# Scores of the global queries made once a batch from a ring of four key tiles, with a builder that counts TensorE's instruction records and with new ranks of the tasks

## The chip, the cores and the metric

The kernel runs on one core of one Trainium2 chip. The core has five engines that run their own instruction lists and wait for each other through semaphores: TensorE (PE in the profile; its weight loads are PEld), VectorE (DVE), ScalarE (ACT), GpSimd (POOL) and SyncE (SP), which here issues all the DMAs. PE writes into PSUM, eight banks of 128 partitions by 512 fp32 numbers; the other data lie in SBUF. The metric is the device time of one execution in microseconds (us).

## The reference

The reference computes attention and then two feed-forward layers on its output:

```python
# attention: batch 4, heads 8, 512 local rows, 32 global rows, head size 64
s_g   = scale * q_g @ concat(k_g, k_l).T            # 32 global queries see all 544 keys
out_g = softmax(s_g) @ concat(v_g, v_l)
s_ll  = where(|i - j| <= 32, scale * q_l @ k_l.T, -1e9)   # local queries: a band ...
s_l   = concat(scale * q_l @ k_g.T, s_ll)                 # ... and the 32 global keys
out_l = softmax(s_l) @ concat(v_g, v_l)
x = concat(out_g, out_l)                            # 2176 rows of 512
# layer 1: rms norm, then (silu(x @ w_gate) * (x @ w_val)) @ w_out, inner size 1536
# layer 2: (sigmoid(x @ w_gate2) * (x @ w_val2)) @ w_out2
```

The weights come as 64-bit floats and are turned into pairs of fp16 numbers (a high and a low part) on the chip.

## The kernel before, in words

The 512 local rows of each batch are four tiles of 128 rows, so there are 16 tiles, T = 0 to 15. A tile goes through a chain of tasks. SP loads its queries, keys and values (`lq`, `lk`, `lv`). PE transposes keys and queries (`k`, `q`), and ACT or DVE copies them out of PSUM into the tile's `kT` and `qT` (`kc`, `qc`). PE makes the banded scores (`a1`: 8 products with a mask, 32 score products of 128 columns), DVE takes the maxima (`mx`), ACT the exponentials (`ex`), PE transposes them (`a2`), ACT or DVE copies them (`pc`), PE multiplies with the value windows `vw` (`a3`, 16 products for each half of the heads), DVE divides (`nm`), ACT, POOL and DVE normalise (`sq`, `ms`, `sc`), PE transposes once more (`a4`), and `xh`, `xl` split the result into the fp16 tiles `xhi`, `xlo`. Each task from `mx` to `nm` exists twice for a tile, for the even and the odd heads (e = 0, 1).

The global queries need every tile of their batch. Before, `st_sg` makes, tile by tile, 16 fp32 products of 64 columns (20 in the last tile of a batch, four of them with the global keys), taking the even and the odd heads in turn; `st_sgc` copies the two results into an SBUF tile `sg`. After the fourth tile `g1` takes the maximum of the whole row on DVE, `g1x` the exponential and the sum on ACT, and `g2`, `gc`, `g3`, `gn`, `gx` transpose, copy, multiply with the values, divide and write to `xG`. The key tiles `kT` come from a pool of three buffers.

The matrix products of layer 1 are cut into pieces of six (`gemm`; tile `wgv` holds gate and value weights, `wo` the output weights). The first two of its twelve weight groups run during attention, as pieces between the attention tasks. A piece needs its three tiles' `xl` and the converted weights. All later products come after attention in a fixed order.

The order on each engine is set when the program is built. `attend` keeps a clock for each engine (`now`), and `book` adds a cost for each instruction. `choose` looks at all tasks whose predecessors have been issued, takes the engine with the earliest possible start, and on it, among those that can start within a short look-ahead (`LOOK`), the task with the lowest rank: a number in units of tiles that is written into `tile_tasks`, `batch_tasks` and `W_PRIO`. A piece of a product has rank 1000, so it stands behind every attention task that can start. Where the builder's clock shows PE waiting for more than `FILL` = 500 ns, it puts in products that nobody uses, fillers (`b<-ident 128x256` in bf16), one for each 110 ns. On the chip each engine executes its list strictly in order, so a task that was put too early holds up everything behind it.

Of the kernel before, what the change touches and what calls it, by code (L numbers as in the profile page):

```python
# [21 lines left out]
def tile_attention_moe_moe(  # L22
# [21 lines left out]
    def tag_of(x):  # L44
        n = x.tensor.name
        return (n, x.offset) if n.startswith(("xhi", "xlo", "ya")) else n
# [13 lines left out]
    mode = [None]  # L60

    class Booked:
# [4 lines left out]
        def __getattr__(self, name):  # L67
            f = getattr(self.eng, name)

            def g(*args, **kw):  # L70
# [5 lines left out]
                if key == "e":  # L76
                    if ins[0].dtype == F32:
                        c = 109 if out.shape[0] == 128 and n == 128 else 18
                    else:
                        c = n / 2.4 + 2.5  # L80
# [4 lines left out]
                    book("e", [out], ins, c, 200)  # L85
# [16 lines left out]
                else:  # L102
                    data = [kw[k] for k in ("in_", "in0", "in1") if k in kw]
                    sb = bool(data) and all(x.space == bass.MemoryType.SB for x in data)
                    if key == "d":
                        c = 75 + (0.52 if sb and len(data) < 2 and "axis" not in kw else 1.04) * n
                    elif key == "a":
                        c = 100 + 0.83 * n + 90 * (kw.get("bias") is not None) + 190 * ("accum_out" in kw)
                    else:
                        c = 60 + (1.95 if len(data) > 1 else 1.05 if data else 0.4) * n + (250 if n == 1 else 0) + 200 * (len(data) > 1)  # L110
                    outs = [out] + ([kw["accum_out"]] if "accum_out" in kw else [])
                    ins = [x for x in ins if x is not kw.get("accum_out")]
                    book(key, outs, ins, c, 85, sb and key != "a")
# [684 lines left out]

    q_t, k_t = {}, {}
    kT, qT = {}, {}  # L800
    sg_t, vt_t, vg_t = {}, {}, {}
    s_t, pt_t, x_t = {}, {}, {}
    g_t = {}
# [52 lines left out]
    def vw_eng(T, n):  # L856
        if T > 1:
            return "s" if n < 2 or n > 5 else "p"
# [20 lines left out]
    def new_kT(T):  # L879
        b, t = divmod(T, TPB)  # L880
        kT[T] = ap.tile([128, NPR, 256], F32, tag="kT", name="kT", bufs=3)
# [4 lines left out]
        if t == 0:  # L886
            nc.gpsimd.memset(gdst[:, :, KB["p"]], 0.0)
        if t == TPB - 1:
# [31 lines left out]
    def st_sg(T):  # L920

        b, t = divmod(T, TPB)
        if t == 0:
# [11 lines left out]
        for e, p in enumerate(ps2):  # L935
            p_t["sg", T, e] = p[:, 0:n]

    def st_sgc(T, e, eng):
        b, t = divmod(T, TPB)
        p = p_t.pop(("sg", T, e))  # L940
        copy(eng, sg_t[b][:, e, t * 128:t * 128 + p.shape[-1]], p)
# [108 lines left out]
    def st_g1(b):  # L1050
        sg = sg_t[b]
        mx = ap.tile([128, 2], F32, tag="gmx", name="gmx")
        den = ap.tile([128, 2], F32, tag="gden", name="gden")
        nc.vector.tensor_reduce(out=mx, in_=sg, axis=AX.X, op=ALU.min)
        g_t[b] = mx, den

    def st_g1x(b, e):
        sg = sg_t[b]
        mx, den = g_t[b]
        nc.scalar.activation(out=sg[:, e], in_=sg[:, e], func=AF.Exp, scale=-1.0,  # L1060
                             bias=mx[:, e:e + 1], accum_out=den[:, e:e + 1])

    def st_g2(b, e):
        sg = sg_t[b]
# [29 lines left out]
    def st_gn(b, e):  # L1094
        p = p_t.pop(("g", b, e))
        if e == 0:
            den = g_t[b][1]
            nc.vector.tensor_scalar(out=den, in0=den, scalar1=1e-9, scalar2=None, op0=ALU.add)
            nc.vector.reciprocal(out=den, in_=den)
# [38 lines left out]

    class Task:
# [451 lines left out]
```

## Time and profile before

| | |
|---|---|
| median of 3 runs | 917.01 us (913.74 to 920.29) |
| the profiled execution | 913.14 us |
| its span, first to last instruction | 911.3 us |
| PE busy | 887.1 us, 97% |
| DVE, ACT, POOL busy | 636.2, 366.9, 286.6 us |
| mean granted PE clock | 0.996 of full speed |

The span is 1.84 us shorter than the time of the execution it is taken from. A busy share is an average over stages with different limits. Attention with the first layer's first products fills the first 203 us; after that PE has only fp16 products.

### The profile page before, as it was taken

What the parts mean: (1) busy time and instruction counts of PE and PEld (TensorE: products, weight loads), DVE (VectorE), ACT (ScalarE), POOL (GpSimd) and SP (SyncE); (2) the same over time, 40 slices, a digit from 0 to 9 for tenths busy, and PEclk for the clock granted to TensorE, in tenths of its full rate; (3) what the DMA queues carried; (4) which work ended last, traced back from release to release, by engine and by line L of the source; (5) the groups of instructions that cost most, each with busy time, mean ns of one, the idle gap of its engine ahead of it and who ended that gap; (6) DMA issues with size and microseconds to landing.
All of it is one profiled execution on the core that took longest, in us unless ns stands there. A gap on an engine that the chain in (4) does not pass through costs nothing.

```text
span 911.3 us, 19662 instructions
## 1 busy us (share of the span) xinstructions
PE 887.1 (97%) x8321; PEld 564.7 (62%) x8321; DVE 636.2 (70%) x927; ACT 366.9 (40%) x687; POOL 286.6 (31%) x327
## 2 busy tenths in 40 slices
PE   9899989899999999999999999999999999999998
PEld 7677666666667667666666666656556565556553
DVE  5786876773766557968958786778778477785352
ACT  4566666655433224313424345444543133322120
POOL 6244452424334542122123424342211303212020
PEclk9998999999999999999999999999999999999999
DMA  9988796630301111200210030130422002000102
GB/s 211 185 197 159 159 177 166 155 97 1 112 29 47 47 47 37 81 24 8 89 44 1 26 110 5 47 93 13 127 64 76 1 1 88 28 1 1 70 24 104
DMA packets 94183, 67.20 MB, mean 74 GB/s; under 512 B 59280, under 2 KB 84368, under 8 KB 94096
## 3 DMA queue, kind: packets, MB, share of 16 engines
q1 hardware_dynamic: 94096, 65.95, 28.4%
q8 instruction: 65, 1.06, 0.5%
q14 instruction: 22, 0.18, 0.1%
HBM read 52.17 MB, written 4.46 MB: 62 GB/s over the span
## 4 chain that ended last, share of the span: by engine, by line
PE 89%; DVE 4%; issue 3%; POOL 2%; ACT 1%; DMA 1%; SPq 0%; POOLq 0%; ACTq 0%; DVEq 0%
PE p L114 59%; PE b L114 31%; DVE wf L114 1%; POOL vw L114 1%; DVE x L114 1%; ACT pt L114 1%; POOL ms L114 1%; DMA vt<-in_v_l_dram 0%; DVE ya L114 0%; DVE G L114 0%; DVE xlo L114 0%; DVE V L114 0%; ACT s L114 0%; POOL kT L114 0%; DVE mx L114 0%
## 5 line engine op out<-in xcount | busy, mean ns | idle before, releaser
L114 PEld LDWEIGHTS <-wc 128*128 128x128 f16 x2304 | 225.3, 98 | 130.2 <-DVE V L114 0.6
L114 PE MATMUL p<-xhi,wc 128*128 128x384 f16 (+1 forms) x768 | 200.8, 317 | 0.0
L114 PE MATMUL p<-tt,wc 128*128 128x384 f16 (+1 forms) x1152 | 200.5, 317 | 0.3 <-DVE V L114 0.3
L114 POOL TENSOR_TENSOR h<-V,h 128x768 f16<-128x768 f32 (+1 forms) x48 | 76.8, 1621 | 272.3 <-ACT h L114 257.6
L114 PE MATMUL b<-xhi,wgv 128*128 128x384 f16 (+1 forms) x576 | 140.2, 317 | 0.3 <-ACT pt L114 0.3
L114 PE MATMUL p<-wo,h 128*128 128x512 f16 x612 | 133.4, 379 | 0.0
L114 PE MATMUL p<-xlo,wc 128*128 128x384 f16 (+1 forms) x384 | 121.7, 317 | 0.0
L114 DVE SCALAR_TENSOR_TENSOR wf<-raw,wf 128x512 int32<-128x512 int32 x144 | 114.2, 802 | 2.2
L114 PEld LDWEIGHTS <-wo 128*128 128x128 f16 x864 | 84.3, 98 | 47.7 <-issue 0.2
L114 PEld LDWEIGHTS <-wgv 128*128 128x128 f16 x864 | 83.4, 98 | 46.2 <-issue 0.2
L114 PEld LDWEIGHTS <-h 128*128 128x128 f16 x612 | 59.9, 98 | 71.0
L114 PE MATMUL b<-xlo,wgv 128*128 128x384 f16 (+1 forms) x288 | 91.3, 317 | 0.0
L114 DVE SCALAR_TENSOR_TENSOR ya<-p,ya 128x768 f32<-128x768 f32 (+3 forms) x42 | 42.4, 1018 | 67.7 <-PE p L114 67.7
L114 ACT ACTIVATE h<-V 128x1536 f16<-128x1536 f32 (+3 forms) x30 | 36.9, 1231 | 102.2 <-DVE V L114 102.2
L114 ACT ACTIVATE sa<-p 128x384 f32<-128x384 f32 (+1 forms) x48 | 22.6, 470 | 118.3 <-PE p L114 101.4
L114 PE MATMUL b<-hhi,wo 128*128 128x384 f16 (+1 forms) x288 | 70.0, 317 | 0.0
L114 PE MATMUL p<-h,wo 128*128 128x384 f16 (+1 forms) x432 | 67.3, 317 | 0.0
L114 ACT ACTIVATE wf<-raw 128x512 f32<-128x512 f32 x72 | 47.5, 671 | 43.8 <-DVE wc L114 23.2
L114 DVE TENSOR_TENSOR V<-p,V 128x768 f32<-128x768 f32 (+3 forms) x72 | 56.6, 786 | 12.2 <-PE p L114 10.1
L114 DVE TENSOR_TENSOR G<-p,G 128x768 f32<-128x768 f32 (+3 forms) x72 | 56.5, 785 | 7.3 <-PE p L114 5.4
L114 POOL TENSOR_TENSOR hlo<-t,hhi 128x384 f16<-128x384 f32 (+1 forms) x36 | 35.6, 990 | 82.0 <-ACT hhi L114 81.8
L114 POOL COPY vw<-vt 32x520 f32<-32x520 f32 (+1 forms) x61 | 42.7, 701 | 40.4 <-PE b L114 17.9
(125 smaller groups left out, 1138.7 us busy)
## 6 DMA issues: line engine op xcount, KB each, us to landing
raw<-in_moe_w_gate_dram SPq DMA_DIRECT2D x24, 512.0 KB, 3.6
raw<-in_moe_w_val_dram SPq DMA_DIRECT2D x24, 512.0 KB, 3.5
raw<-in_moe_w_out_dram SPq DMA_DIRECT2D x24, 512.0 KB, 3.5
vw<-vt SPq DMA_DIRECT2D x28, 260.0 KB, 6.5
k<-in_k_l_dram SPq DMA_DIRECT2D x16, 256.0 KB, 6.1
q<-in_q_l_dram SPq DMA_DIRECT2D x16, 256.0 KB, 5.4
vt<-in_v_l_dram SPq DMA_DIRECT2D x32, 128.0 KB, 4.3
out_dram<-ya SPq DMA_DIRECT2D x16, 256.0 KB, 2.1
```

Of the source, the lines that this page charges most:

```text
L114: return f(*args, **kw)
```

## The change

There are three parts. The key tiles of a batch now lie in one tile `kTr` with a place for each of the four tiles, and the next batch writes into the same places. `st_sg` is called for a batch and a half of the heads: 8 products of 256 columns (64 columns of each of the four tiles at once) and 4 products of 32 columns with the global keys, into two banks. The maxima are taken from these banks, and ACT reads them there for the exponential and writes into a free part of `yacc[2]`, so that the copies and the tile `sg` are gone. New predecessors go with it: the keys of a batch's tiles wait for both score tasks of the batch before (`guard` puts this wait in front of PE's transposes, too).

The builder's account gets a second clock for PE: every 256 records of its instruction list (four for an fp32 product, two for any other) must have come before they can run, and a task whose records have not come is taken to start later. Costs of several instructions are set anew.

The ranks of all tasks are moved into one table `PR`, with other numbers. The same goes for the weights' ranks, and POOL's look-ahead is 100 in place of 200.

```diff
+    def fetch(n):
+        n_pe[0] += n
+        while 256 * len(came) + 138 <= n_pe[0]:
+            t = max([now["e"]] + came[-1:])
+            came.append(t + 2550 + max(1300, min(0.8 * (now["dma"] - t), 4500)))
+        now["e"] = max(now["e"], fetched(0))
+
+    def fetched(n):
+        i = (n_pe[0] + n - 450) // 256
+        return came[min(i, len(came) - 1)] if i >= 0 else 0.0
...
                 if key == "e":
+                    fetch(4 if ins[0].dtype == F32 and name == "matmul" else 2)
...
+    kTr = const.tile([128, TPB, NPR, 256], F32, name="kTr")
+    sgx = yacc[2][:, 1280:1280 + 2 * (SL + SG)].rearrange("p (e s) -> p e s", e=2)
...
-    def st_sg(T):
-
-        b, t = divmod(T, TPB)
-        if t == 0:
-            sg_t[b] = ap.tile([128, 2, SL + SG], F32, tag="sg", name="sg", bufs=1)
-        ps2 = [bank(("sgc", T, e)) for e in range(2)]
-        kv = kT[T].rearrange("p r (a c) -> p r a c", c=32)
-        n = 160 if t == TPB - 1 else 128
-        for pr in range(NPR):
-
-            for m, k in enumerate((kv[:, pr, 0:4:2], kv[:, pr, 4:8:3], kgT[:, pr, b * SG:(b + 1) * SG])[:n // 64 + n % 64 // 32]):
-                for e, p in enumerate(ps2):
-                    nc.tensor.matmul(p[32 * pr:32 * pr + 32, 64 * m:min(64 * m + 64, n)],
-                                     qgT[64 * e:64 * e + 64, pr, b * SG:(b + 1) * SG], k[64 * e:64 * e + 64],
-                                     start=True, stop=True)
...
+    def st_sg(b, e):
+
+        p, pg = [bank(("g1x", b, e)) for _ in range(2)]
+        kv = kTr.rearrange("p t r (a c) -> p t r a c", c=32)
+        r = slice(64 * e, 64 * e + 64)
+        for m in range(3):
+            for pr in range(NPR):
+                if m < 2:
+                    k = kv[r, :, pr, (0, 4)[m]:(4, 8)[m]:m + 2]
+                    o = p[32 * pr:32 * pr + 32].rearrange("p (t a) -> p t a", t=TPB)[:, :, 64 * m:64 * m + 64]
+                else:
+                    k, o = kgT[r, pr, b * SG:(b + 1) * SG], pg[32 * pr:32 * pr + 32, 0:SG]
+                nc.tensor.matmul(o, qgT[r, pr, b * SG:(b + 1) * SG], k, start=True, stop=True)
+        p_t["sg", b, e] = p, pg[:, 0:SG]
...
     def st_g1x(b, e):
-        sg = sg_t[b]
         mx, den = g_t[b]
-        nc.scalar.activation(out=sg[:, e], in_=sg[:, e], func=AF.Exp, scale=-1.0,
-                             bias=mx[:, e:e + 1], accum_out=den[:, e:e + 1])
+        for i, (x, c) in enumerate(zip(p_t.pop(("sg", b, e)), (slice(0, SL), slice(SL, SL + SG)))):
+            nc.scalar.activation(out=sgx[:, e, c], in_=x, func=AF.Exp, scale=-1.0,
+                                 bias=mx[:, e:e + 1], accum_out=den[:, 2 * i + e:2 * i + e + 1])
...
+    PR = dict(lkg=-1.55, kgt=-0.88, lqg=1.98, qgt=1.14, gB=0.54, lk=-1.6, lq=-0.85, lv=-0.68, lg=-0.17, q=-0.13, qc=-0.53, k=-0.82,
...
+    N_PE = {"a1": 144, "a3": 64, "sg": 48, "g3": 160, "g2": 10}
...
-        task(("kc", T), KC, lambda e: st_kc(T, e), P(-1.1 if t else -0.65), ("k", T), ("nk", T), ("nk", T + 1) if t < TPB - 1 else None,
-             c=(1040, 1100))
...
+        task(("kc", T), "ad" if PR["kcd"] else "a", lambda e: st_kc(T, e), P(PR["kc" if t else "kc0"]), ("k", T), ref("a1", T - TPB),
+             ref("a1", T - TPB + 1) if t < TPB - 1 else None, ref("sg", b - 1, 0), ref("sg", b - 1, 1), c=(1040, 1100))
...
+                    if e == "e":
+                        n = N_PE.get(t.key[0], 8)
+                        x = max(x, fetched(n) - 8 * n)
```

The numbers in `PR` tell little by themselves; the lists that come out of them show what moved. On PE before, at the turn from the first batch to the second (`ident,k`, `ident,q`, `ident,x`, `ident,s` are transposes of keys, queries, results and exponentials; `vw,pt` is `a3`; `vt,ptg` and `vg,ptg` are `g3`; `kT,qgT` is `st_sg`):

```order
L114 MATMUL b<-ident,s 128x128 x4
L114 MATMUL b<-vw_88,pt 32x65 x16
L114 MATMUL b<-vt,ptg 32x64 x16
L114 MATMUL b<-vg,ptg 32x64 x4
L114 MATMUL b<-vw_88,pt 32x65 x16
L114 MATMUL b<-kT,qgT 32x64 x16
L114 MATMUL b<-ident,q 128x128 x4
L114 MATMUL b<-vt,ptg 32x64 x16
L114 MATMUL b<-vg,ptg 32x64 x4
L114 MATMUL b<-ident,k 128x128 x4
L114 MATMUL b<-kT,qgT 32x64 x16
L114 MATMUL b<-ident,x 128x128 x4
```

On PE after, in the second batch, from the second half of its score products on (`kTr,qT` is `a1`; `wgv` starts a piece of layer 1):

```order
L128 MATMUL b<-kTr,qT 32x128 x32
L128 MATMUL b<-kTr,qgT 32x4x64 x8
L128 MATMUL b<-kgT,qgT 32x32 x4
L128 MATMUL b<-ident,x 128x128 x4
L128 MATMUL b<-ident,s 128x128 x4
L128 MATMUL b<-vw_89,pt 32x65 x32
L128 MATMUL b<-ident,s 128x128 x4
L128 MATMUL b<-ident,q 128x128 x4
L128 LDWEIGHTS wgv
L128 MATMUL b<-xhi_73,wgv 128x384
```

The small products of one tile's scores, of the batch's scores and of the global rows no longer stand in one row; each batch has two short blocks of 12 score products, and pieces of layer 1 lie between.

On DVE before, where tile 1's maxima stand among the conversion of the first value weights (`wf`, `wgv`):

```order
L114 SCALAR_TENSOR_TENSOR wgv<-wf,wgv 128x2x512
L114 TENSOR_SCALAR wf<-wf 128x512
L114 SCALAR_TENSOR_TENSOR wf<-raw,wf 128x512 x2
L114 TENSOR_SCALAR wf<-wf 128x512
L114 SCALAR_TENSOR_TENSOR wf<-raw,wf 128x512 x2
L114 TENSOR_REDUCE mx<-b 128x4 x2
L114 SCALAR_TENSOR_TENSOR wgv<-wf,wgv 128x2x512
```

On DVE after, at the same place (`gmx<-b` are the maxima of the first batch's global scores):

```order
L128 SCALAR_TENSOR_TENSOR wgv<-wf,wgv 128x2x512
L128 TENSOR_SCALAR wf<-wf 128x512
L128 SCALAR_TENSOR_TENSOR wf<-raw,wf 128x512 x2
L128 TENSOR_REDUCE mx<-b 128x4 x2
L128 TENSOR_REDUCE gmx<-b 128x1 x2
L128 TENSOR_TENSOR gmx<-gmx 128x1
L128 TENSOR_REDUCE mx<-b 128x4 x2
L128 TENSOR_REDUCE gmx<-b 128x1 x2
```

Tile 1's maxima moved ahead of the second half of these weights, and the global maxima came in; the 24 copies into `sg` are gone from the lists.

Counted over the lists: PE's fillers are 158 instead of 220, in both cases all ahead of the first piece of layer 1. That piece stands behind the fourth tile's scores (before: the fifth's). When the last transpose of attention is issued, 216 + 72 products of layer 1 are done (before 228 + 72). The weight conversions on DVE and ACT up to the end of attention are the same in number.

## Rows read from the trace of the kernel before

**Rows 1.** The page: span, busy times, DMA queue of instructions.

```profile
span 911.3 us, 19662 instructions
...
PE 887.1 (97%) x8321; PEld 564.7 (62%) x8321; DVE 636.2 (70%) x927; ACT 366.9 (40%) x687; POOL 286.6 (31%) x327
...
q8 instruction: 65, 1.06, 0.5%
```

**Rows 2.** Stretches: length, busy PE, PEld, DVE, ACT, POOL, clock, DMA share, GB/s.

```profile
0.00:203.00 203.00, 183.46 (x3973) 139.45 (x3973) 149.09 (x313) 125.67 (x351) 84.32 (x172) 0.98 0.79 168
203.00:911.30 708.30, 703.68 (x4348) 425.30 (x4348) 487.11 (x614) 241.24 (x336) 202.27 (x155) 1.00 0.15 47
```

**Rows 3.** Waits of PE up to 420 us: us in total, times, longest.

```profile
PE b L114 <- issue: 12.7, 8, 2.5
PE b L114 <- DVE x L114: 1.4, 1, 1.4
```

**Rows 4.** Timeline of PE, a run of fillers and what follows: start us, us.

```profile
8.19 2.46 PE L114 MATMUL b<-ident 128*128 128x256 bf16 x21
10.48 0.60 PE L114 MATMUL b<-ident,k 128*128 128x128 f32 x4
```

**Rows 5.** Groups by form, the fillers: busy us, mean ns.

```profile
L114 PE MATMUL b<-ident 128*128 128x256 bf16 x220 | 26.8, 273 | 0.0
```

**Rows 6.** Timeline of PE at a wait for issue, third batch.

```profile
106.62 0.66 PE L114 MATMUL b<-vw,pt 128*32 128x65 f32 x32
107.22 0.52 PE L114 MATMUL b<-kT,qgT 64*32 64x64 f32 x32
107.66 0.66 PE L114 MATMUL b<-ident,q 128*128 128x128 f32 x4
108.25 0.66 PE L114 MATMUL b<-vt,ptg 128*32 128x64 f32 x32
108.84 0.32 PE L114 MATMUL b<-vg,ptg 32*32 32x64 f32 x8
109.08 0.44 PE L114 MATMUL b<-kT,qgT 64*32 64x64 f32 x20
110.99 0.43 PE L114 MATMUL b<-kT,qgT 64*32 64x64 f32 x12 [1.46 <-issue]
```

**Rows 7.** DMAs of the first 203 us, the queue of instructions: packets, MB.

```profile
q8 instruction: 31, 0.51, 1.2%
```

**Rows 8.** Timeline of PE, banded scores, values and a transpose of queries.

```profile
163.56 1.13 PE L114 MATMUL b<-kT,qT 64*32 64x128 f32 x64
164.62 0.67 PE L114 MATMUL b<-vw,pt 128*32 128x65 f32 x32
165.22 0.66 PE L114 MATMUL b<-ident,q 128*128 128x128 f32 x4
```

**Rows 9.** The same columns for the stretch at half the PE clock.

```profile
72.20:79.00 6.80, 6.80 (x196) 5.52 (x192) 4.17 (x10) 3.76 (x14) 1.50 (x7) 0.50 0.20 47
```

**Rows 10.** Timeline of DVE: the maxima of tile 1, the last step of tile 2.

```profile
34.77 1.28 DVE L114 TENSOR_REDUCE mx<-b 128x4 f32<-128x512 f32 x2
...
58.90 0.68 DVE L114 TENSOR_TENSOR xlo<-b,xhi 128x512 f16<-128x512 f32 x1
```

**Rows 11.** Timeline of PE: the first piece of layer 1.

```profile
60.36 0.34 PE L114 MATMUL b<-xhi,wgv 128*128 128x384 f16 x1
```

**Rows 12.** Groups by form on DVE and ACT: maxima, score copies, key copies.

```profile
L114 DVE TENSOR_REDUCE mx<-b 128x4 f32<-128x512 f32 x32 | 21.3, 683 | 2.3 <-PE b L114 2.3
...
L114 ACT ACTIVATE kT<-b 128x256 f32<-128x256 f32 x32 | 10.6, 389 | 4.6 <-PE b L114 4.5
...
L114 DVE TENSOR_REDUCE gmx<-sg 128x2 f32<-128x1088 f32 x4 | 5.1, 1277 | 0.0
...
L114 DVE COPY sg<-b 128x128 f32<-128x128 f32 x18 | 4.4, 284 | 2.5 <-PE b L114 2.5
```

**Rows 13.** DMA issues on the page: KB each, us to landing.

```profile
k<-in_k_l_dram SPq DMA_DIRECT2D x16, 256.0 KB, 6.1
```

More of the change, by code (lines that the diff above doesn't have):

```diff
@@ L60, in tile_attention_moe_moe @@
     mode = [None]
+    n_pe = [0]
+    came = []
+    def fetch(n):
[7 more added lines that the diff above has]
+        return came[min(i, len(came) - 1)] if i >= 0 else 0.0
     class Booked:
@@ L84, in g @@
                         mode[0] = m
-                    book("e", [out], ins, c, 200)
+                    book("e", [out], ins, c, 215)
                 elif key == "s":
@@ L797, in tile_attention_moe_moe @@
     vw = [const.tile([128, 4, H * DV], F32, name=f"vw{i}") for i in range(2)]
+    kTr = const.tile([128, TPB, NPR, 256], F32, name="kTr")
+    sgx = yacc[2][:, 1280:1280 + 2 * (SL + SG)].rearrange("p (e s) -> p e s", e=2)
     q_t, k_t = {}, {}
-    kT, qT = {}, {}
-    sg_t, vt_t, vg_t = {}, {}, {}
+    kT = {T: kTr[:, T % TPB] for T in range(NT)}
+    qT = {}
+    vt_t, vg_t = {}, {}
     s_t, pt_t, x_t = {}, {}, {}
@@ L1097, in st_gn @@
             den = g_t[b][1]
-            nc.vector.tensor_scalar(out=den, in0=den, scalar1=1e-9, scalar2=None, op0=ALU.add)
-            nc.vector.reciprocal(out=den, in_=den)
+            nc.vector.scalar_tensor_tensor(out=den[:, 0:2], in0=den[:, 0:2], scalar=1e-9, in1=den[:, 2:4], op0=ALU.add, op1=ALU.add)
+            nc.vector.reciprocal(out=den[:, 0:2], in_=den[:, 0:2])
             g_t["x"] = ap.tile([128, 2, D], F32, tag="xg", name="xg", bufs=1)
@@ L1208, in batch_tasks @@
+        task(("a4", T), "e", lambda e: tr4(("x", T), x_t.pop(T), ("xl", T)), P("a4"), ("sc", T), banks=1)
+        task(("xh", T), "ad", lambda e: st_xh(T, e), P("xh"), ("a4", T), c=(525, 607))
+        task(("xl", T), "d", lambda e: st_xl(T), P("xl"), ("xh", T))
     def batch_tasks(b):
-        P = lambda x: TPB * b + TPB - 1 + SGP + 0.02 * x
-        task(("g1", b), "d", lambda e: st_g1(b), P(1), *[("sgc", TPB * b + t, e) for t in range(TPB) for e in range(2)])
+        P = lambda x: TPB * b + TPB - 1 + PR["g"] + 0.02 * x
@@ L1211, in batch_tasks @@
         for e in range(2):
-            task(("g1x", b, e), "a", lambda _, e=e: st_g1x(b, e), P(2), ("g1", b))
+            task(("sg", b, e), "e", lambda _, e=e: st_sg(b, e), TPB * b + TPB - 1 + PR["sg"] + 0.1 * e, *[("kc", TPB * b + t) for t in range(TPB)],
+                 ("qgc",), banks=2)
+            task(("g1", b, e), "d", lambda _, e=e: st_g1(b, e), P(1), ("sg", b, e))
+            task(("g1x", b, e), "a", lambda _, e=e: st_g1x(b, e), P(2), ("g1", b, e), ref("g2", b - 1, 0), ref("g2", b - 1, 1))
@@ L1251, in post @@
     def post(key, engs, f, *deps, c=None):
-        task(("post", *key), engs, f, -1, *deps, c=c)
+        task(("post", *key), engs, f, PR["post"], *deps, c=c)
     n_post = [0]
@@ L1322, in gemm_out @@
         for d in range(4):
-            yield [h_post[g, ch, j] for j in range(2)], lambda: w_done[g][1], 1
+            yield [h_post[g, ch, j] for j in range(2)] + [("g2", B - 1, e) for e in range(2) if q == 2], lambda: w_done[g][1], 1
             n_out[0] += 1
@@ L1340, in tile_attention_moe_moe @@
     last_ch = {g: [w[1] for w in work if w[0] == g][-1] for g in range(2)}
-    W_PRIO = {0: 0.95, 1: 0.96, 2: 2.0, 3: 12, 4: 13, 5: 14, 6: 16, 7: 16.5, 8: 18}
-    LOOK = {"e": 150, "d": 200, "a": 500, "p": 200, "s": 100}
-    BACKLOG = 4000
-    FILL = 500
+    W_PRIO = {n: PR["w%d" % n] for n in range(9)}
+    LOOK = {e: PR["L" + e] for e in "eadps"}
+    BACKLOG, FILL = PR["backlog"], PR["fill"]
     ready = {}
@@ L1400, in choose @@
             r = last.get(h[-3], 0.0) if len(h) > 2 else 0.0
[L1401 removed]
+            cand.setdefault("s", []).append((max(now["s"], now["dma"] - BACKLOG, r), (W_PRIO.get(w_pos[0] // 2, 50) + PR["raw"], 0), "R"))
         best = None
@@ L1432, in attend @@
                 ops.pop(0).f()
-                ready[key] = now[e] + 85
+                ready[key] = now[e] + 130
             else:
@@ L1465, in run_op @@
         if e:
-            ready[key] = now[e] + 85
+            ready[key] = now[e] + 130
     def give():
```

112 lines of the change are left out of this document (54 added, 58 removed).

## The prediction, made before the run

> **What bounds the kernel now.** I read the page first, then the busy times by stretch, then what PE waited for, then PE's timeline around those waits. PE is busy for 887.1 of 911.3 us [rows 1], so only PE's own time can shrink the span. By stretches the slack lies in one place: up to 203 us PE is busy for 183.46 us, and after that for 703.68 of 708.3 us [rows 2]. DVE (149.09 of 203 us) and ACT (125.67) are not full in attention. So PE's time is work, plus fillers, plus idle time, and since the work must be done anyway, the change is worth what it takes from the other two.
>
> Fillers: 220 in the first stage [rows 5]; 21 of them take from 8.19 to 10.48 us, 0.109 us each [rows 4], so 220 × 0.109 = 24.0 us. Idle time: 203 − 183.46 = 19.5 us. Of it 12.7 us in eight pieces carry the name "issue", a wait for nothing that the profile shows; the longest wait for another engine is 1.4 us [rows 3]. The remaining 6.8 us are the start and small waits for engines.
>
> What "issue" is can be read from two numbers. The queue of instructions brings 65 blocks of 16 KB, and PE has 8321 products and 8321 weight loads; 65 × 256 = 16640 [rows 1]. So a block holds 256 records of PE, and 31 blocks came in attention [rows 7]. The wait that ends at 110.99 us began at 109.53, and since 106.62 PE had run 128 products with their 128 weight loads, exactly one block, in 2.9 us [rows 6]. After attention a product takes 703.68 / 4348 = 0.162 us [rows 2], a block of them 20.7 us, and no such wait is left. So PE runs dry where 256 records are used up faster than the next block comes, which is among small fp32 products.
>
> **The change part by part.**
>
> *Fewer fillers.* 62 go: 62 × 0.109 = 6.8 us. A filler covers a gap that the builder expects, so this is a gain only if the gap is gone. The lists say why it could be: the first piece of layer 1 stands one tile earlier, and DVE makes tile 1's maxima three weight instructions earlier. These began at 34.77 us, and the first piece ran at 60.36, right behind tile 2's last step at 58.90 to 59.58 [rows 10, 11]; what comes off this chain comes off the fillers. Bounds: 0 (all come back as idle time) and 6.8; I take 6.8, because beside the fillers PE waited for engines only little (6.8 us in all).
>
> *Fewer waits for records.* The score products were 16 × 16 + 4 × 8 = 288 instructions of four records (the trace shows each as two products with two loads), and now 4 × 24 = 96. That is 768 records less, with the fillers' 124 together 892, or 3.5 of 31 blocks. More weight has the order. I went through both lists at the pace of the rows (0.109 a filler, 0.15 a transpose [rows 6], 1.06 / 32 = 0.033 a banded score and 0.60 / 16 = 0.0375 a value product [rows 8], 0.44 / 16 = 0.0275 an old global score [rows 6]) and took the time of the 256 records ahead of each place where a block runs out. Under 4.5 us were 11 of them before and are 3 after; under 4 us 9 and 1. Bounds: no gain, since a block also took longer in places (the DMA engines were busy 79% of the stage [rows 2]), and 12.7 us, all of it. The first waits, while nothing but attention can run, should stay. I take 3 of the 8, some 5 us: a gain of 7.7.
>
> *The score products themselves.* The columns are the same, 64 × 256 for 256 × 64. At the old price per column they cost the same, 7.9 us in all. But the old list took even and odd heads in turn, the two halves of the array's rows, and a task of the new list stays in one half. Bounds: the banded scores' price, 0.033 for 128 columns, gives 64 × 0.066 + 0.9 = 5.1 us (2.8 less); products that run one after another, at a transpose's 0.15 for 128 columns, give 64 × 0.30 = 19 us (11 more). The nearest row is that of the value products: they too keep their rows and change only the column group, and cost 0.0375 for 65 columns, so 64 × 0.148 + 32 × 0.0375 = 10.7 us or 2.8 more, with a load for every 65 columns, where the new ones have one for 256. I take +1.
>
> [...]
>
> *What DVE and ACT lose and gain.* 24 copies of some 284 ns and four maxima of 1277 ns go; 16 maxima come, eight of them of 512 columns like the tiles' own at 683 ns [rows 12]. DVE gains some 3 us in all. Both engines have room in attention, so I count nothing. If that cover were gone, it would be a gain of these 3 us.
>
> *Ring and guards.* PE's transposes of a new batch's first keys now wait for both score tasks of the batch before, and so does everything queued behind them on PE; the loads of later keys on SP wait for those transposes in turn. In the list the transposes stand behind two `a2` and two `a3` blocks or a piece of layer 1, so I count nothing; the price without cover is in the rivals.
>
> *A tighter order.* The old builder did not know of the waits for records, so on the chip PE came later than planned, and other engines had that time in hand. Now it is planned away. Bounds 0 and the 6.8 us of such idle time there are now, once more; I take 1.5.
>
> [...]
>
> *After attention* the same products follow in the same order, 12 of them moved from before the end of attention (no change in the sum), and as many weights are converted by then.
>
> Sum: 911.3 − 6.8 − 7.7 + 1 + 1.5 = 899.3 us of span; with the 1.84 us around it 901.1. The profiled execution was 913.14 us and the median of the runs 917.01, so the runs may lie up to 4 us higher than this; I let the range carry that.
>
> **The rivals.**
>
> *The waits for records stay.* The blocks could come as late as before wherever the small products stand, since the DMA engines are as full. For it: in the first part of attention, before any piece of layer 1 can run, little changes. Against it: 11 places become 3. Then 911.3 − 6.8 + 1 + 1.5 + 1.84 = 909.
>
> *The new products run one after another*, because they stay in one half of the rows. For it: nothing in the old list did this. Against it: the value products. Then 901 + 10 = 911.
>
> *The ring stops PE at the turns of the batches.* The place is the transposes of keys of tiles 4, 8 and 12, behind the score tasks. If a key load is late there, a turn costs the transposes (0.6 us), ACT's copies (2 × 0.389 and two smaller ones, 1.4 us [rows 12]) and the landing of the next keys (6.1 us [rows 13]), 8 us; three turns 24 us, so 925. It decides when the loads behind the guard land later than the work that stands between lasts. For it: PE takes its list in order, and in the first batch only fillers could stand there. Against it: two buffers of keys are loaded ahead, and blocks of `a3` and pieces of layer 1 stand between. From about 4 us a turn on the gain is gone.
>
> *More is won*: the clock stays up (−3.4) and the waits for records shrink to two of eight, 3.2 us (−9.5): 911.3 − 6.8 − 9.5 − 3.4 + 1 + 1.84 = 894; without half of the 6.8 us of small waits 891.
>
> **How the numbers follow.** Forecast 901 with 0.55, its own range 893 to 908; waits for records stay 0.20; products one after another 0.06; ring 0.11; more won 0.08. The forecast is the likeliest case. The range must leave out no more than 2 in 10: from 888, the better case with its bounds, to 915, which takes in both milder rivals and the 4 us between the profiled execution and the median, and leaves out the ring. A measurement of this kernel, whose runs are up to 0.7% apart, can tell about 1% from no change: below 907.8 is faster, above 926.2 slower. Of the forecast 0.48 fall below, of the waits that stay 0.06, of more won all 0.08: 0.62. Of the ring 0.07 lies above, and I add 0.02 for other waits; the rest, 0.29, is the same.
>
> **What would show it.** In the profile after: 158 fillers, the last before about 50 us; waits for issue of about 5 us in some three places instead of 12.7 in eight; 61 or 62 instruction blocks; the new score products at 0.11 to 0.15 us each; the end of attention some 13 us earlier; no wait of PE for a single engine above 2 us. It is wrong if PE waits for ACT or DVE where fillers stood, if the waits for issue stay above 10 us, or if PE stands ahead of the transposes of keys at a batch's turn.

## The result and the profile after

The changed kernel takes 905.53 us (median of 6 runs, 902.66 to 909.83), beside 915.98 for the kernel before (6 runs, too): ratio 0.989, 95% interval 0.9854 to 0.9925. The profiled execution took 905.0 us with a span of 903.2. Two slow runs of the kernel before (923.27 and 923.71 us) are left out of the ratios, the means and the line below.

The page of the changed kernel, for [rows 1]:

```profile
span 903.2 us, 18734 instructions
...
PE 878.9 (97%) x7875; PEld 556.7 (62%) x7875; DVE 632.2 (70%) x922; ACT 367.4 (41%) x697; POOL 288.1 (32%) x320
...
q8 instruction: 62, 1.02, 0.5%
```

The span lost 8.1 us and PE's busy time 8.2, so the idle time is what it was: 24.3 us after, 24.2 before. This one subtraction already says that the idle time did not shrink by the waits for records that I had counted on. The stretches up to the end of attention (193.47 us now, 203 before) and behind it, for [rows 2]:

```profile
0.00:193.47 193.47, 173.64 (x3518) 130.68 (x3519) 144.84 (x306) 126.56 (x361) 86.77 (x164) 0.99 0.83 175
193.47:903.20 709.73, 705.23 (x4359) 425.98 (x4357) 487.33 (x617) 240.85 (x336) 201.38 (x156) 1.00 0.15 47
```

All of it comes off the first stretch; the second grew by 1.4 us, since 12 products more are left for it. The fillers, for [rows 5], and PE's waits up to 420 us, for [rows 3]:

```profile
L128 PE MATMUL b<-ident 128*128 128x256 bf16 x158 | 19.7, 273 | 0.3 <-DVE x L128 0.3
```

```profile
PE b L128 <- issue: 4.1, 5, 1.6
PE b L128 <- DVE x L128: 3.8, 6, 1.1
PE b L128 <- ACT s L128: 2.2, 4, 1.1
PE b L128 <- DMA k<-in_k_l_dram: 2.1, 1, 2.1
PE b L128 <- DMA q<-in_q_l_dram: 1.5, 1, 1.5
```

Waits for issue fell from 12.7 to 4.1 us. All other rows of this view together (engines and DMAs) rose from 6.5 to 15.9, 3.6 of these 9.4 us in the two rows for DMAs, which the kernel before did not have. One row that shrinks proves nothing until the others are added up.

The time came from the start. DVE's and PE's timelines of the changed kernel, for [rows 10, 11]:

```profile
30.87 1.29 DVE L128 TENSOR_REDUCE mx<-b 128x4 f32<-128x512 f32 x2
...
50.90 0.69 DVE L128 TENSOR_TENSOR xlo<-b,xhi 128x512 f16<-128x512 f32 x1
```

```profile
47.83 1.47 PE L128 MATMUL b<-ident 128*128 128x256 bf16 x12
...
51.61 0.33 PE L128 MATMUL b<-xhi,wgv 128*128 128x384 f16 x1
```

The maxima of tile 1 begin 3.9 us earlier, the third tile's last step 8.0, and the first piece of layer 1, right behind it as before, 8.75. PE's idle time ahead of that piece is nearly unchanged (6.6 us before, 6.9 after), though the waits for issue in it fell from 4.1 to 0.8 us. What is gone is busy time: 6.8 us of fillers, and 2.3 us of attention's work that now stands behind the piece, which is no gain. The last of the 158 fillers end at 49.30.

The stretch at half the clock (0.50) now takes 3.4 us, again behind a wait, that for the keys of tile 8 (2.08 us; in the kernel before, the stretch began 1.8 us after a wait of 2.52):

```profile
76.00:78.40 2.40, 0.32 (x4) 0.11 (x2) 1.70 (x3) 2.40 (x8) 2.20 (x4) 1.00 1.17 201
...
79.70:83.10 3.40, 3.40 (x98) 2.59 (x104) 1.47 (x7) 0.18 (x2) 2.16 (x5) 0.50 1.25 181
```

Before it took 6.8 us [rows 9]. Four transposes of keys in it, from 72.68 us on, took 1.11 us, beside 0.60 at full clock [rows 4]; if all the work at 0.50 took about twice as long, 1.7 us of PE's time come from here, an estimate. The account of the profiled span: fillers −62 × 0.109 = −6.8, clock −1.7 (this estimate), idle +0.1, all else +0.3, together −8.1.

### The profile page after: what moved, and what is told of

It is laid out like the page before. It is cut to its first block, busy times and chain, and to the rows that moved or that the text cites. A ratio compares the mean times of both kernels' runs of the same rounds, so it can differ in the third digit from the quotient of the medians.

```text
span 903.2 us, 18734 instructions
## 1 busy us (share of the span) xinstructions
PE 878.9 (97%) x7875; PEld 556.7 (62%) x7875; DVE 632.2 (70%) x922; ACT 367.4 (41%) x697; POOL 288.1 (32%) x320
## 3 DMA queue, kind: packets, MB, share of 16 engines
q8 instruction: 62, 1.02, 0.5%
## 4 chain that ended last, share of the span: by engine, by line
PE 90%; DVE 3%; ACT 2%; DMA 2%; issue 1%; POOL 1%; SPq 1%; ACTq 0%; POOLq 0%; DVEq 0%
PE p L128 61%; PE b L128 28%; DVE x L128 1%; POOL ms L128 1%; ACT pt L128 1%; DMA k<-in_k_l_dram 1%; SPq L128 1%; ACT s L128 1%; DMA q<-in_q_l_dram 1%; DVE mx L128 0%; DMA vt<-in_v_l_dram 0%; DVE wf L128 0%; DVE vw L128 0%; DVE ya L128 0%; ACT ya L128 0%
## 5 line engine op out<-in xcount | busy, mean ns | idle before, releaser
L128 DVE SCALAR_TENSOR_TENSOR wf<-raw,wf 128x512 int32<-128x512 int32 x144 | 112.3, 788 | 2.1
L128 POOL COPY vw<-vt 32x520 f32<-32x520 f32 (+1 forms) x61 | 47.2, 775 | 53.4 <-PE b L128 34.5
```

The costliest lines, as they stand in the source:

```text
L128: return f(*args, **kw)
```

## The clock in the timed runs

Runs of one kernel differ in good part by the granted clock. The 80 runs of the kernel before that stand beside the experiments, by their mean granted clock (mean time, number of runs; five of the eleven values that occur), with the changed kernel's six:

```
clock     0.991       0.994       0.996       0.998       1.000
before    919.6 (9)   915.9 (20)  914.2 (15)  910.8 (12)  911.1 (1)
after                 909.8 (1)               905.4 (4)   904.4 (1)
```

A line through the 80 falls by 1.02 us for each 0.001 of clock (correlation −0.73, so it accounts for about half of the variance); by the estimate above 0.001 is 1.8 of 911 us at 0.50 and costs 0.9 us, which agrees. The kernel before had 0.9945 on the mean of the 80, the changed one 0.9977: 3.3 us of the 10.4. At 0.998 the two stand 5.4 us apart. So the gain has two parts, 5 to 7 us at the same clock and 3 to 5 of clock. Whether the second part belongs to the change is open: e13_widea below has the changed kernel's order and had 0.9936. For the experiments I read both, the time and the mean clock.

## The experiments

In the table "other" is the sum of all rows but issue in PE's waits up to 420 us, "fillers" counts all of them, "first piece" is the start of the first piece of layer 1 in us, "low" the time at the lower clock in the profiled execution (0.50 in the two main traces), "clock" the mean over the timed runs (for the kernel before, over the 80). The experiments ran in three groups (e1 to e4, e5 to e9, e10 to e13), each on a chip of its own beside runs of the kernel before (medians 916.2, 915.3 and 915.3 us). The changed kernel was not run again with them, so differences to it are between medians of different groups. Each row of waits rests on one profiled execution.

```
                 median  ratio to before           span   PE busy idle  issue other fillers first  low   clock
                                                                                            piece
before           916.0   1                         911.3  887.1   24.2  12.7   6.5  220     60.36  6.8   0.9945
after            905.5   0.989  [0.9854, 0.9925]   903.2  878.9   24.3   4.1  15.9  158     51.61  3.4   0.9977
e1_clock         919.4   1.0034 [1.0011, 1.0057]   918.0  887.8   30.2  17.0   6.9  219     60.73  3.4   0.9959
e2_noclock       913.5   0.9958 [0.9928, 0.9987]   910.7  881.6   29.1   1.5  22.9  160     51.96  6.8   0.9950
e3_oldranks      923.8   1.0082 [1.0049, 1.0115]   917.9  884.5   33.4  10.4  18.7  181     58.73  6.8   0.9926
e4_pool          916.5   1.0002 [0.9978, 1.0025]   912.9  885.1   27.8   6.5  15.8  226     54.11  3.4   0.9947
e5_nofill        913.4   0.9984 [0.9955, 1.0014]   912.7  871.1   41.6   7.9  28.8    0     51.89  23.8  0.9836
e6_lat           912.2   0.9972 [0.9947, 0.9998]   911.6  883.6   28.0  15.0   8.3  182     60.75  10.2  0.9954
e8_noring        927.2   1.0145 [1.0095, 1.0195]   927.5  887.8   39.7  11.0  24.1  167     60.81  10.2  0.9938
e9_ramp          917.0   1.0028 [0.9999, 1.0058]   913.5  882.3   31.2   4.0  22.5  174     55.25  6.8   0.9946
e10_weights      917.0   1.0029 [0.9999, 1.0059]   916.7  887.4   29.3  14.8   9.1  189     59.02  6.8   0.9950
e11_noadd        902.1   0.9862 [0.9824, 0.9901]   901.5  881.0   20.5   2.1  13.3  158     50.88  6.8   0.9977
e12_wide         911.2   0.9957 [0.9928, 0.9986]   906.6  885.9   20.7  10.9   4.9  104+12  57.37  3.4   0.9966
e13_widea        909.9   0.9943 [0.9913, 0.9973]   904.6  879.5   25.1   9.5  11.1  74+10   51.92  3.4   0.9936
```

**e1_clock.** The kernel before with the account of records alone.

```
...
+                    fetch(4 if ins[0].dtype == F32 and name == "matmul" else 2)
...
+                    if e == "e":
+                        n = N_PE.get(t.key[0], 8)
+                        x = max(x, fetched(n) - 8 * n)
```

> The kernel before with one thing added, the builder's clock for PE's records of 256. Scores tile by tile, ranks and costs are those of before. Its list has 219 fillers (220) and 7 places instead of 11 where a block of records would be used up in under 4.5 us. Theory 1, that the waits for issue go where the list spreads the small products: these waits fall from 12.7 us to about 8, and the time is 0.3 to 0.6% under before. Rival, that the clock is worth nothing without the new ranks and the ring: waits for issue above 11 us, time within 0.2% of before.

Slower by 0.34%, not faster, and the waits for issue rose to 17.0 us in 14 pieces. The account of records has no worth of its own on the old ranks; theory 1 fell, and the rival's "within 0.2%" was too narrow as well.

**e2_noclock.** The changed kernel without that account.

```
     def fetch(n):
-        n_pe[0] += n
+        return
```

> The changed kernel with that clock switched off; ring, ranks and costs stay. 160 fillers (158), 5 places under 4.5 us (3). Theory 1: waits for issue rise from 4.1 to 6 to 8 us, waits for named engines fall a little, time 0.2 to 0.4% above the changed kernel. Rival, that the fewer records of the ring do it alone: waits for issue stay at 4 to 5 us and the time is the same as that of the changed kernel.

Some 0.7% slower than the changed kernel (8 us, of which some 3 are clock), more than either theory gave. The waits:

```profile
PE b L128 <- DVE x L128: 7.8, 9, 1.9
...
PE b L128 <- issue: 1.5, 4, 0.5
```

The waits for issue fell, where the account against them was taken out, and the others rose to 22.9 us; both theories had them rise or stay. The first piece stayed at 51.96: the account of records doesn't make the early start. The loss lies behind it, in an order that differs there.

**e3_oldranks.** Ring and accounts as changed, ranks as before.

```
-    PR = dict(... mx=0.19, ex=-0.18, a2=-0.12, pc=-0.7, ... w0=0.66, ...)
+    PR = dict(... mx=-0.03, ex=-0.06, a2=-0.09, pc=-0.12, ... w0=0.95, ...)
```

> The changed kernel with the ranks of before (ring, clock and new costs stay). 181 fillers, 7 places under 4.5 us. Theory 1 gives 23 fillers more (2.5 us) and some 4 us more of waits for issue: 0.6 to 0.8% above the changed kernel, so nearly the time of before. Rival, that ranks are indifferent as long as PE has pieces to put in between: within 0.2% of the changed kernel.

About 1.9% slower than the changed kernel (some 5 of the 18 us are clock), with the first piece at 58.73, though only 0.7 us of waits for issue are left ahead of it. Ring and accounts without the ranks lose, and by more than either theory gave.

**e4_pool.** The changed kernel with POOL's costs booked as before.

```
-  c = 60 + ... + (120 if n == 1 else 0) + 85 * (len(data) > 1)
+  c = 60 + ... + (250 if n == 1 else 0) + 200 * (len(data) > 1)
```

> The changed kernel with two of the builder's costs for POOL as before (250 and 200 ns in place of 120 and 85): the step ms, which the trace shows at 222 + 572 ns, was booked at some 450 ns by the change and is booked at some 820 here. Theory 2, that this cost makes PE's transposes of the results stand too early: PE's waits for DVE x (3.8 us) and DVE's waits for POOL ms (8.6 us) fall below half. The list has 226 fillers, since the ranks were made for the other cost. If fillers are time lost, 68 more cost 7.4 us, and it is 0.5 to 0.8% slower than the changed kernel; if they only stand where PE would wait anyway, it is as fast or up to 0.4% faster.

The waits of PE for DVE's `x` did not halve but went from 3.8 to 5.0 us, so theory 2 fell. Of the 68 fillers more, 49 stand behind the first piece (80 to 168 us) and only 19, or 2.1 us, ahead of it; the first piece moved by 2.5. At 1.2% it is slower than either case of the expectation.

**e5_nofill.** The changed kernel without fillers. As fillers count in the account of records, the order moves in places too.

```
-              ... backlog=4000, fill=500, ...
+              ... backlog=4000, fill=1000000, ...
```

> The changed kernel without any filler (158 of 0.109 us, 17.2 us, left out; their results are used by nothing). Theory 1 (the fillers only stand where PE would otherwise wait, and the time is set by when DVE and ACT have the operands of the first piece of layer 1): PE's idle time rises from 24.3 to about 41 us, the first piece still starts at 50 to 53 us, and the time is within 0.5% of the changed kernel's 905.5 us, ratio to before 0.985 to 0.993. Theory 2 (fillers are time taken from PE): up to 17 us less, ratio about 0.972. [...]

The first piece (51.89) did not move, as theory 1 has it: the fillers stood where PE had nothing to do. But the clock was down for longer, and the time rose by 7.9 us, beyond the 0.5% of theory 1. The page's PE and clock rows (40 slices of 22.8 us), and two stretches:

```profile
PE   6688887999999999999999999999999999999998
...
PEclk9799989999999999999999999999999999999999
```

```profile
25.50:32.30 6.80, 5.57 (x101) 4.15 (x107) 6.63 (x10) 4.60 (x11) 2.94 (x6) 0.53 1.00 232
...
0.00:203.00 203.00, 166.54 (x3365) 120.23 (x3366) 150.72 (x312) 126.12 (x358) 82.57 (x164) 0.94 0.80 169
```

The lower clock took 23.8 us instead of 3.4, in five stretches, three of them in the first 46 us, where PE is busy for some six tenths of each slice. Where the 17.2 us of fillers went is seen by cutting the span at the first piece. Ahead of it PE is busy for 35.06 us instead of 44.73, or 7.5 us more for the same work without the fillers, and idle for 16.8 instead of 6.9, 9.9 us more: the slower work took the rest of the place that fillers had, and cost nothing. Behind it the run is 9.2 us longer, some 7.4 of them idle time and 1.9 busy time. So here the fillers in their place cost nothing, and with them the clock was down for 3.4 us instead of 23.8. What the loss behind the first piece owes to the lower clock and what to the moved order, this run doesn't separate.

**e6_lat.** 100 ns more booked behind each instruction.

```
-                    book("e", [out], ins, c, 215)
+                    book("e", [out], ins, c, 315)
...
-                    book(key, outs, ins, c, 130, sb and key != "a")
+                    book(key, outs, ins, c, 230, sb and key != "a")
```

> The changed kernel with 100 ns more booked behind each instruction of PE, DVE, ACT and POOL in the builder's account (182 fillers instead of 158). Theory 1 (the waits for engines, 15.9 us, come from an order planned too tight): they fall to about 8 us, the 24 fillers more take back 2.6, and the time is 1 to 5 us lower than the changed kernel's. Theory 2 (idle time and fillers only change places, since the chain through DVE and ACT sets the time): waits for engines fall by no more than the fillers add, and the time is the same or up to 4 us higher.

```profile
PE b L128 <- issue: 15.0, 9, 3.6
PE b L128 <- DVE x L128: 3.0, 6, 1.2
```

The waits for engines halved as theory 1 wanted, from 15.9 to 8.3, but those for issue rose from 4.1 to 15.0, the first piece fell back to 60.75, and the time rose by 6.7 us (some 2 of them clock), beyond the 4 that theory 2 allowed. Theory 2 in the trace, in the main: they changed places. As the order is another one and the first piece later, it is no clean exchange.

**e8_noring.** Scores tile by tile as before, with the changed accounts and ranks (but for the ranks `nk` and `g`, which are those of before).

```
...
+        task(("sg", T), "e", lambda e: st_sg(T), P(1.2), ("kc", T), ("qgc",), ...)
...
+            task(("sgc", T, e), "ad", lambda eng, e=e: st_sgc(T, e, eng), T + 1.2, ("sg", T), ...)
...
-            task(("sg", b, e), "e", lambda _, e=e: st_sg(b, e), TPB * b + TPB - 1 + PR["sg"] + 0.1 * e, ...)
```

> The changed kernel with its account, costs and ranks, but the global queries' scores made tile by tile again (288 products instead of 96, three key buffers instead of the ring, 24 copies to DVE or ACT; 167 fillers). Theory 1 (the ring itself is worth little, the gain of the change is in the order of the first 60 us): 1 to 5 us slower than the changed kernel, 906 to 910, ratio to before 0.990 to 0.995, waits for issue up by about 4 us for three blocks more. Theory 2 (the ring with its 768 records less is most of the gain): 913 to 918, ratio 0.997 to 1.003.

21.7 us slower than the changed kernel, more than either theory gave. Some 4 us of that are clock. Records alone can't be it: waits for issue rose by 6.9 us, and the others by 8.2, with the first piece at 60.81. The ranks fit the ring and nothing else, so this run shows what the old scores cost under these ranks, not what the ring is worth by itself. A ring of two batches, which would need no guards, is untested.

**e9_ramp.** The ranks of loads and first weights as before, those of the attention steps as changed.

```
-    lqg=1.98, qgt=1.14, gB=0.54, lq=-0.85, lv=-0.68, lg=-0.17, ... lk1=0.37, ... raw=0.0, w0=0.66
+    lqg=0.6, qgt=0.9, gB=0.7, lq=-1.0, lv=-0.8, lg=-0.5, ... lk1=0.0, ... raw=-0.3, w0=0.95
```

> The changed kernel with the ranks of the loads and of the first weights set back to those of before (global queries, values, gains, the first weight pieces and their conversion); the ranks of the attention steps stay (174 fillers). Theory 1 (the ranks' worth of about 1.9% lies in the ramp, in which loads and weights stand ahead of the first piece): the first piece starts at 54 us or later and the time is 4 us or more above the changed kernel's. Theory 2 (it lies in the ranks of the attention steps): first piece by 53 us, time within 3 us of the changed kernel's.

```profile
55.25 0.34 PE L128 MATMUL b<-xhi,wgv 128*128 128x384 f16 x1
```

The first piece starts 3.6 us later and the time is 11.5 us above the changed kernel's; some 3 us of that are clock (0.9946). Both conditions of theory 1 are met, but the ramp is the smaller part: of the 10.3 us that the span grew, 3.6 lie ahead of the first piece and the rest behind it, nearly all of this rest idle time (6.9 us more in all, 0.8 of them ahead). The ranks of loads also place the loads of later tiles.

**e10_weights.** The kernel before with the weights' conversions ranked 0.1 later.

```
-                    pr = W_PRIO.get(3 * ops[0].g + ops[0].w, 50)
+                    pr = W_PRIO.get(3 * ops[0].g + ops[0].w, 50) + 0.1
```

> The kernel before with one number changed: the ranks of the weights' conversion 0.1 later, so that DVE makes the maxima of tile 1 ahead of weight instructions (189 fillers instead of 220). Theory 1 (the gain lies in the ramp: DVE's part of the third tile ends earlier, and with it the first piece of layer 1 starts earlier): the first piece starts at 53 to 57 us instead of 60.36, right behind the third tile's last step, and the time is 3 to 7 us lower, ratio to before 0.992 to 0.997. Theory 2 (a better ramp is given back later as idle time, without the other parts): ratio 0.998 to 1.005.

A miss. The list had the first piece much earlier, the chip only by 1.3 us. 31 fillers less (3.4 us; 19 of the 189 now stand behind the first piece) came with 5.1 us more idle time, 2.8 of it ahead of the first piece, and with 14.8 us of waits for issue. Putting DVE's maxima ahead of the weights is not what shortens the start, at least not by itself.

**e11_noadd.** The changed kernel in the same order, with the addition ahead of POOL's power left out and its time still booked.

```
-        nc.gpsimd.tensor_scalar(out=ms, in0=ms, scalar1=1e-6, scalar2=None, op0=ALU.add)
+        book("p", [ms], [ms], 181.05, 130, True)
```

> The changed kernel without POOL's addition of 1e-6 ahead of its power in the normalization of each tile (17 instructions of 0.22 us; this small constant is left out of the computation), in the same order on every engine. Theory 1 (the idle time is the chain through POOL and DVE: DVE waited 8.6 us in 10 pieces for POOL there): DVE's waits fall by some 2 to 2.5 us, PE's waits for engines by 1.5 to 2.5, and the time by 1 to 2.5 us. Theory 2 (the records take its place): waits for issue grow by what the waits for engines lose, and the time stays within 0.5 us.

DVE's wait for POOL's `ms` in the changed kernel:

```profile
DVE x L128 <- POOL ms L128: 8.6, 10, 1.7
```

and in this one, with PE's largest rows:

```profile
DVE x L128 <- POOL ms L128: 3.5, 5, 1.1
...
PE b L128 <- issue: 2.1, 4, 0.8
...
PE b L128 <- DVE x L128: 0.9, 3, 0.3
```

DVE's wait fell by 5.1 us, more than the 17 × 0.22 = 3.7 us taken out; PE's wait for `x` fell from 3.8 to 0.9, and the idle time from 24.3 to 20.5, though 3.4 us more at the lower clock took back 1.7. Here the waits for issue did not grow. The median is 3.4 us below the changed kernel's at the same mean clock; the intervals of the two overlap, but the rows that got shorter are those of this chain. This is theory 1, with more gain than it gave: by these traces some 3.8 us of the idle time were the chain from one engine to the next.

**e12_wide** and **e13_widea.** The fillers with 512 columns instead of 256, in the unchanged order, on the kernel before and on the changed one: 208 and 148 records less.

```
-                    for i in range(int((gap - FILL / 2) / 110)):
+                    two = one.unsqueeze(1).to_broadcast([128, 2, 256])
+                    n = int((gap - FILL / 2) / 110)
+                    for i in range(n // 2):
+                        nc.tensor.matmul(p.rearrange("p (a c) -> p a c", a=2), one[:, 0:128], two, start=True, stop=True)
+                        now["e"] += 2.5
+                    if n % 2:
                         nc.tensor.matmul(p[:, 0:256], one[:, 0:128], one, start=True, stop=True)
```

On the changed kernel `fetch(2)` stands behind the line with 2.5, so that the builder goes on counting as many records as with two fillers.

> The kernel before with its 220 fillers of 256 columns made as 104 of 512 and 12 of 256: the same filler time, 208 records less, the same order on every engine. Theory 1 (waits for issue come from records used up faster than they come; fewer records in the first 60 us shift them away, and the engines' results are there in time): waits for issue fall from 12.7 to 8 to 10 us, and the time by 2 to 4. Theory 2 (waits for issue and for engines change places): the waits for issue fall as much, waits for engines rise by as much, and the time is within 1 us of before.

> The changed kernel with 74 fillers of 512 columns and 10 of 256 in place of 158 of 256, in the same order on every engine: 148 records less. Theory 1 as for the kernel before: waits for issue fall from 4.1 to 1 to 3 us and the time by 1 to 3, ratio to before 0.985 to 0.988. Theory 2: the time is within 1 us of the changed kernel's, the waits for issue shift elsewhere or turn into waits for engines.

On the kernel before:

```profile
PE b L114 <- issue: 10.9, 9, 3.6
```

```profile
57.37 0.34 PE L114 MATMUL b<-xhi,wgv 128*128 128x384 f16 x1
```

Same order, first piece 3.0 us earlier, idle time down by 3.5, nearly all of it ahead of that piece (6.6 to 3.2 us); time 4.1 us lower, of which some 2 are clock (0.9966 for 0.9945). The waits for issue fell by 1.8 us only, less than theory 1 gave, but the other waits fell too. Ahead of the first piece the waits for issue fell from 4.1 to 0.9 us, which is the 3 us. So records do cost time in the first 60 us. On the changed kernel, whose order was made for the old number of records:

```profile
PE b L128 <- issue: 9.5, 9, 3.4
PE b L128 <- DVE x L128: 5.1, 8, 1.2
```

148 records less, and waits for issue up from 4.1 to 9.5, the others down from 15.9 to 11.1, the first piece and the span nearly the same. The places where a block runs out were moved off the places that the order had kept for them (8 blocks were used up in under 4.5 us, 3 on the changed kernel), which fits what the account of records is meant to do; and moving them cost nothing here, because what PE doesn't wait for records it waits for engines. The median is 4.4 us higher, which the clock accounts for: at 0.998 and 1.000 it took 906.4 and 904.1 us, the changed kernel 905.4 and 904.4. Why the wide fillers had a lower clock on this kernel (0.9936) and a higher one on the other stays open.

## Why the prediction was right, step by step

The time came out near the forecast partly by luck: one term was 6.3 us too hopeful, and 2.4 us of others made up for a part of it.

*Fewer fillers*, −6.8: right in size and condition. There are 158 fillers, and no idle time in their place ahead of the first piece. The number of fillers is only the sign of the gain: e5 shows that fillers that are merely left out leave the first piece where it was. The gain is that this piece starts 8.75 us earlier, less the 2.3 us of work that moved behind it.

*Fewer waits for records*, −7.7, and *a tighter order*, +1.5: the first was right as a sum (12.7 to 4.1 us in five pieces, 5 in three forecast; 62 blocks) and wrong as a gain, and the second is the term that was mis-sized: the waits for engines and DMAs grew by 9.4 us, not 1.5. I had written myself that the other engines had the time of those waits in hand, and bounded the term by the 6.8 us of small waits. The right bound was the 12.7 us themselves: when PE comes earlier to a chain that is not earlier, it waits for the chain. e13 shows the exchange in the other direction and in an unchanged order (−4.8 against +5.4), e6 in another order (−7.6 against +10.9), and e11 shows that a shorter chain ends it. On the order before there is no such exchange: in e12 both kinds of waits fell. That all of the 9.4 us are exchange is not shown; 3.6 of them are waits for loads.

The reading of "issue" as the end of a block holds, and the trace shows it more firmly than my one place, whose rows add up to 132 products, not 128. Counted from PE's first record in each trace (weight loads, products, and its own semaphore and drain records), 87 of the 89 waits for issue of over 0.25 us in the fourteen traces come at the same remainder by 256, that is at the end of a block. But the places were not the ones I counted. Of the kernel before's eight such waits only five end a block that was used up in under 4.5 us, out of ten such blocks. The changed kernel has three, as counted in the list, and only one of them (4.0 us) ends in a wait, of 1.6 us; its three other waits of over 0.25 us end blocks of 4.9 to 7.5 us. So that the sum came out near 5 us is luck in part.

*The score products*, +1: a task's 8 products of 256 columns and 4 of 32 now take 0.89 and 0.17 us:

```profile
65.50 1.07 PE L128 MATMUL b<-kTr,qgT 64*32 64x256 f32 x16
...
66.39 0.24 PE L128 MATMUL b<-kgT,qgT 64*32 64x32 f32 x8
66.56 0.34 PE L128 MATMUL b<-xhi,wgv 128*128 128x384 f16 x1
```

Eight such tasks are 8.5 us beside 7.9: +0.6. A product of 256 columns takes 0.111 us, the lower end of what I gave, though the whole task stays in one half of the rows. The rival that they run one after another is refuted by 0.111 beside 0.30 us.

*The clock*: the forecast counts no change of it. No run shows the 3.4 us that the better case takes for a clock that stays up; the runs showed the 6.8 us at 0.50 [rows 9] become 3.4, by the estimate above 1.7 us in the profiled execution, and 3.3 us on the mean of the runs. Of the forecast span (899.3) the chip missed 3.9 us: 6.3 too much gain from records, less 1.7 of clock, less 0.7 because all else cost 0.3 instead of 1.

*Ring and guards*, 0: PE stood once at a batch's turn, 2.08 us ahead of the keys of tile 8. By my own signs that counted against the forecast, but it is not the mechanism of the rival. SP's and PE's timelines of the changed kernel:

```profile
71.71 0.58 SPq L128 DMA_DIRECT2D k<-in_k_l_dram  x1
```

```profile
78.39 0.63 PE L128 MATMUL b<-ident,k 128*128 128x128 f32 x4 [2.08 <-DMA k<-in_k_l_dram]
```

The load of these keys needs one of two buffers, which tile 6's transposes, begun at 59.95, had read last; the guard does not hold it, and the score tasks that guard the transposes had ended by 70.3. SP issued it only at 71.71, right behind loads of queries and values, and it landed at 78.25. The kernel before issued the same load at 65.64, though its first piece came later. So this wait comes from the place of the load in SP's new list; whether the ring had a part in putting it there is open. e8 says that the ring can't be taken out of this kernel, so "counted at nothing" holds for its waits, not for its part in the order.

*DVE and ACT*, and *after attention*, 0: DVE is busy 4.0 us less, which shows nowhere in the span; the second stretch is 1.4 us longer with 12 products more.

Of the rivals, "waits for records stay" came as near in time (909) with the wrong mechanism: the waits went, and their worth went to other waits. Of my signs, attention ended 9.5 us earlier instead of 13, and the longer waits for DVE and ACT were among the signs of being wrong: both go with the mis-sized term.

What stays open: which of the ranks make the start earlier. e3 and e9 show that the ranks do, those of loads and first weights for 3.6 of 8.75 us; e2 shows that the account of records does not; e10 that one plausible swap alone does not either. Waits for records are a rival for a part: ahead of the first piece they fell from 4.1 to 0.8 us, and e12 shows such a fall moving the piece by 3.0 us on the old order; against it, e3 has only 0.7 us of them there and the piece at 58.73. No run separates the ring's worth from ranks that fit it.

## What to carry to other kernels

Add up all waits of an engine before counting the fall of one row as a gain: a wait that vanishes is worth only what the next operand's engine is ahead of it (here the waits for issue fell by 8.6 us, and the others rose by 9.4). Where idle time is made up by fillers, look for the step that ends the filling (here the third tile's last step on DVE); the fillers themselves cost nothing here (the first piece began at 51.61 us with them, at 51.89 without), and without them PE stood at the lower clock for 23.8 us instead of 3.4 and the span was 9.5 us longer. Print the granted clock beside each run: 0.001 of it was 1 us here, and the higher clock of its runs was a third of the difference that was measured for this change.

## What the runs showed of the hardware

The granted clock goes with about half of the variance that looks like noise: the same program took 906.8 to 923.1 us, with a mean clock of 0.998 at the lower end and 0.991 at the upper. In the two main traces the fall of the clock to 0.50 followed PE's longest wait of the attention stage, 2.52 us in the kernel before and 2.08 in the changed one.

Waits for issue lasted up to 3.7 us (e8_noring), where the longest of the kernel before was 2.5; 74 fillers made wider moved them from 4.1 to 9.5 us in all (e13_widea). In all fourteen traces the packets of the queue of instructions (60 to 65, of 16 KB; 65 and 62 in the two main traces) are PE's products and weight loads divided by 256, rounded. In attention the waits for issue came to 12.7 us before and up to 17.0 (e1_clock), while behind attention none is left in the two main traces. The faster a block was used up, the more often a wait of over 0.25 us stood at its end, but not each time: over the fourteen traces, 31 of the 38 blocks whose records ran within 3.5 us ended in one, 19 of 48 between 3.5 and 4.5 us, 26 of 116 up to 6 us, and 3 of the 543 that lasted over 8 us.
